# From the third batch on, two Fourier stages as 64x64 tiles of TensorE, eight groups a visit

## The chip, the cores and the metric

One core of one Trainium2 chip runs the whole program. The metric is the device time of one execution in microseconds. For the kernel before, three runs gave 746.88, 747.74 and 748.42 us, median 747.74. The profiled execution of the same kernel took 747.4 us; its span, from the first instruction to the last, is 745.2 us, so 2.2 us lie around it.

## The reference

Eight sequences of 3008 tokens with 256 features are filtered in the frequency domain, and the result goes through a two-layer network.

```
X = np.fft.rfft(x, axis=1)                  # x: (8, 3008, 256)
Y = X * (filt_r + 1j * filt_i)[None]        # filters: (1505, 256)
y = np.fft.irfft(Y, n=3008, axis=1)
h = y.reshape(24064, 256) @ w_in            # w_in: (256, 2048)
g = np.maximum(0.01 * h, h)
out = g @ w_out                             # w_out: (2048, 256)
```

## The kernel before

**The transform.** 3008 is 94 x 32, and each batch goes through four matmul stages in half precision:

- Stage 1 (`s1_group`, 16 groups, L259): a transform of length 94 over the rows, for two of the 32 values of n2 at a time. Its result is copied to half precision by ACT (L262) or DVE and stored in a DRAM scratch, `dz1` (L264).
- Stage 2 (`s2_group`, 12 groups): `t1_load` reads the scratch back, turned (L271), into `z1`, four slots of 128 partitions x 4 columns k1 x 256. Two matmuls of 128x128 weights by 256 columns (L308) fill one PSUM bank `pf`. DVE multiplies the bank by the two filter layouts, `fb_sb` (L317) and `fa_sb` (L320); the two 64-partition halves of the first product are exchanged by two transfers (L318, L319), and POOL adds the products into `y` (L323).
- Stage 3 (`sa_group`, 12 groups): one matmul of 128x128 weights by 512 columns on `y` (L330), copied by ACT (L332) and, after every second group, stored in the scratch `dz2` (L334).
- Stage 4 (`sb_group`, 16 groups): `t2_load` (L278) reads `dz2` back, four matmuls of 94 columns a group (L351), copied by ACT into `yt` (L341).

Batch 0 takes its own route, with DVE transposes in place of the scratch (`FIRST`), and a last part of it runs later (`late_sb`, L442). There, and in L401, weights of 128 rows by 64 columns are used in pairs that write the two halves of the PSUM partitions.

**The network.** The 24064 tokens are 47 chunks of 512. `moe1` multiplies by `w_in` (L514), 16 column tiles a chunk, two to a double bank `ph`; there are two of these, used in turn, and ACT applies the leaky relu and empties them (L519). The second product runs one chunk behind (L589; the first three chunks by L681), from the fourth chunk on by a Winograd-like scheme of seven products of 16 matmuls of 128 columns, with sums before (L555) and after them on DVE.

**The order.** It is written out by the program. Time is counted in units; a chunk is `SL = 8` units, a column tile of `moe1` falls every half unit, and 112 matmuls of the second product are spread evenly over the chunk. `at(time, f)` puts each piece of work into one list, which is emitted in order of time; each engine, and each queue of transfers, then runs in that order and waits only for what it needs. `PLANS` says when the groups of a batch begin and how far apart they are, 47 units a batch from the fourth on. A planner loop moves a group later until what it needs is there, at least `GAP = 0.6` units after the last; `load_time` places the reads back `LANDED = 2.43` units after the last store and `READ = 2.2` units ahead of their first use. The stage groups share two PSUM banks `pf`; the two `out_banks` and the two double banks `ph` belong to the network. SP issues nearly all transfers and runs through its list in order; POOL issues the loads of `x` and, at the start, of the weights and filters, which change from single to half precision on the way.

Units and microseconds: the first `moe1` matmul, at unit 0, starts at 34.27 us of the span; the first stage-4 group of batch 1, at unit 38.52, is at 109.24 us.

Of the kernel before, what the change touches and what calls it, by code (L numbers as in the profile page):

```python
# [11 lines left out]
P = 128  # L12
# [7 lines left out]
N1, N2 = 94, 32  # L20
NC = 24
Q = 32
R1 = 96
FP = 3


def _build_np_constants(N):
    n1, n2 = np.arange(N1), np.arange(N2)
    h = N2 // 2

    k2 = np.concatenate([np.arange(h), np.arange(N2 - 1, h - 1, -1)])

    sg = np.where(k2 < h, 1.0, -1.0)[None, :]
    th = 2 * np.pi * np.outer(n2, k2) / N2
    co, si = np.cos(th), np.sin(th)

    fwd1 = np.zeros((P, P))
    fwd2 = np.zeros((P, NC, P))
    inv1 = np.zeros((P, N2, N1))
    inv2 = np.zeros((P, P))  # L40

    for s, (qr, qi) in enumerate(((0, 2), (1, 3))):
        k1 = NC * s + np.arange(NC)

        cr, ci = (slice(64 * i + s, 64 * i + 64, 2) for i in range(2))
        r, i = (slice(Q * q, Q * q + Q) for q in (qr, qi))
        ang = 2 * np.pi * np.outer(n1, k1) / N1
        fwd1[:N1, qr * Q : qr * Q + NC] = np.cos(ang)
        fwd1[:N1, qi * Q : qi * Q + NC] = -np.sin(ang)
        for c in range(NC):  # L50
            t = th + 2 * np.pi * n2[:, None] * k1[c] / N
            fwd2[r, c, cr], fwd2[i, c, cr] = np.cos(t), np.sin(t)
            fwd2[r, c, ci], fwd2[i, c, ci] = -np.sin(t) * sg, np.cos(t) * sg

        w = np.where((k1 == 0) | (k1 == N1 // 2), 1.0, 2.0)[:, None] / N1
        for j in n2:
            t = ang.T + 2 * np.pi * j * k1[:, None] / N
            inv1[qr * Q : qr * Q + NC, j, :] = w * np.cos(t)
            inv1[qi * Q : qi * Q + NC, j, :] = -w * np.sin(t)
        inv2[cr, r], inv2[ci, r] = co.T, -(si * sg).T  # L60
        inv2[cr, i], inv2[ci, i] = si.T, (co * sg).T
    inv2 /= N2


    inv2r = np.concatenate([inv2[:64], -inv2[:64]], axis=0)
    inv2i = np.concatenate([inv2[64:], inv2[64:]], axis=0)
    small = np.stack([fwd1, inv2, inv2r, inv2i], axis=1)

    fwd2t = fwd2.reshape(4, Q, NC, P).transpose(1, 0, 2, 3).reshape(P, NC, P)
    inv1t = inv1.reshape(4, Q, N2, N1)[:, :NC].transpose(1, 0, 2, 3).reshape(4 * NC, N2, N1)  # L70
    fwd2 = fwd2.reshape(P, FP, NC // FP, P).transpose(1, 0, 2, 3)
    return tuple(np.ascontiguousarray(t).astype(np.float16) for t in (fwd2, inv1, small, fwd2t, inv1t))


@with_exitstack
def kernel(
# [28 lines left out]
    REST = (5.37, 14.61, 8.86, 10.48, 23.53, 20.72)  # L105
    DUE = (3.52, 0.66)
    TWICE = (2.2, 2.35)
    F2T = 3.24
    LEAD = (3.85, 7.37)
    AFTER = (0.53, 0.8, 1.33, 3.17, 0.39, 0.52)  # L110
# [2 lines left out]
    PLANS = (  # L113
        (0.68, 0.31, 12.95, 0.9, 4.35, 38.33, 2.78, 7.78, 1.61),
        (12.19, 1.53, 42.87, 2.62, 7.4, 85.59, 2.85, 16.13, 2.12),
        (40.7, 1.73, 77.28, 3.57, 5.62, 130.03, 2.65, -0.23, 2.52),
        (63.95, 2.85, 119.86, 3.87, 7.04, 177.42, 2.92, 12.93, 2.24),
    )

    f2_np, i1_np, small_np, f2t_np, i1t_np = _build_np_constants(N)  # L120
    f2_d = nc.inline_tensor(f2_np, name="fwd2_const")
    i1_d = nc.inline_tensor(i1_np, name="inv1_const")
    small_d = nc.inline_tensor(small_np, name="small_const")
    f2t_d = nc.inline_tensor(f2t_np, name="fwd2t_const")
    i1t_d = nc.inline_tensor(i1t_np, name="inv1t_const")

    cpool = ctx.enter_context(tc.tile_pool(name="const", bufs=1))
    f2_sb = cpool.tile([P, NC, P], FP16, name="f2_sb")
# [3 lines left out]
    fb_sb = cpool.tile([P, NC, D], FP16, name="fb_sb")  # L132
    w_in_sb = cpool.tile([P, NDT, DFF], FP16, name="w_in_sb")
    w_out_sb = cpool.tile([P, NCT, D], FP16, name="w_out_sb")
    wt_sb = cpool.tile([P, 4, NCH, P], FP16, name="wt_sb")
    x_sb = cpool.tile([P, N2, D], FP16, name="x_sb")
    big = [cpool.tile([P, Q * D], FP16, name=f"big{i}") for i in range(3)]
# [31 lines left out]
    def at(time, f):  # L169
        clock["n"] += 1  # L170
        heapq.heappush(work, (time, clock["n"], f))
# [69 lines left out]
    def turned(t, n, c):  # L241

        base = t[:]
        return bass.AP(tensor=base.tensor, offset=base.offset + 4 * c * D,
                       ap=[[P * D, n], [Q * D, 4], [1, 4 * D]])
# [22 lines left out]
    def t1_load(b, c):  # L268
        def go():
            need(*[("st1", b, h) for h in range(8)], *[("s2", b, 2 * c - 7)] * (c > 3))  # L270
            nc.sync.dma_start(z1[c % 4], turned(dz1[b % 2], N2, c))  # L271
            issued.add(("z1", b, c))
        return go

# [51 lines left out]
    def sa_group(b, g):  # L326
        def go():
            ps = bank("pf", 2, D)
            need(("y", b, g), *[("st2", b, g // 2 - 4)] * (g > 7))
            nc.tensor.matmul(ps, inv2, ys.pop((b, g))[:], start=True, stop=True)  # L330
            h = g // 2
            nc.scalar.copy(st2[h % 4][:, ds(2 * (g % 2), 2), :], ps)  # L332
            if g % 2:
                soon(AFTER[4], lambda: noted(("st2", b, h), lambda: nc.sync.dma_start(  # L334
                    dz2[b % 2][ds(4 * h, 4)].rearrange("k p d -> p k d"), st2[h % 4])))
        return go

    def quad_copy(h, dt, ps, copy):

# [354 lines left out]
    def plan(b, s1, s1_step, s2, s2_step, lag, sb, sb_step, xl, x_step):  # L694
        for g in range(16):
            groups.append((s1 + s1_step * g, 1, b, g, s1_group(b, g, dve if b == 1 and g % 4 < 3 else act)))
            if g % 2 and b + 1 < B:
                at(s1 + xl + x_step * g, lambda g=g: (need(("s1", b, g)), noted(
                    ("x", b + 1, g // 2), lambda: x_load(b + 1, 2 * g - 2, 4))))
        for g in range(12):  # L700
            groups.append((s2 + s2_step * g, 2, b, g, s2_group(b, g)))
            groups.append((s2 + lag + s2_step * g, 3, b, g, sa_group(b, g)))
        first_use[1, b], first_use[3, b] = s2, sb
        for g in range(16):
            due = SL * (QT * (8 * b + g // 2) // CH)
            groups.append((min(sb + sb_step * g, due - DUE[0] + DUE[1] * (g % 2)), 4, b, g, sb_group(b, g, act)))
# [21 lines left out]
    def load_time(stage, b, c):  # L728
# [7 lines left out]
            at(t, (t1_load if stage == 1 else t2_load)(b, c))  # L736
        return loads[stage, b, c]

    queue = [(time, n, *v) for n, (time, *v) in enumerate(groups)]
    heapq.heapify(queue)  # L740
    while queue:
        time, n, stage, b, g, f = heapq.heappop(queue)
        t = max(time, last + GAP)
        if stage == 3:
            behind = when[2, b, g] + y_delay(b, g) + 0.02 if (2, b, g) in when else None
        else:
            behind = load_time(stage - 1, b, g // 2) if stage != 1 else 0
            if stage != 1 and behind is not None:
                behind += READ
# [6 lines left out]
            place[stage - 1, g // 2 % 4] = t + 0.1  # L756
        assert stage < 4 or t < SL * (QT * (8 * b + g // 2) // CH), (b, g, t)

    for ci in range(NCHUNK + 1):
        if ci < NCHUNK:  # L760
            for ct in range(NCT):
                at(SL * ci + 0.5 * ct, lambda ci=ci, ct=ct: moe1(ci, ct))
        if ci == 0:
            continue
        wino = W0 <= ci - 1
# [39 lines left out]
```

## Time and profile before

| what | value | where from |
|---|---|---|
| median of three runs | 747.74 us | the runs |
| profiled execution, its span | 747.4 us, 745.2 us | the profiled run |
| PE busy | 738.0 us, 99% | part 1 of the page |
| DVE, ACT, POOL busy | 504.6, 559.1, 166.2 us | part 1 |
| granted TensorE clock | 0.999 | the spans of the cores |
| leaky relu, L519, 128x1024 | 376 x 1025 ns | groups by form |
| copies of stage 3, L332, 128x512 | 84 x 584 ns | groups by form |
| filter products, L317 and L320, 128x512 | 78 x 688 and 84 x 681 ns | groups by form |
| add of the products on POOL, L323 | 84 x 1388 ns | part 5 |
| load of x, landing after issue | 4.4 us for 192 KB | part 6 |

Busy times of PE are those of the records, whose modelled ends lie after the start of the next matmul; what one matmul costs in a stream is read from start to start. DMA issues on SP and POOL aren't counted as busy.

### The profile page before, as it was taken

Reading aid. Unit: us, or ns where it says so; the run is one execution under the profiler, and the core shown is the slowest. Engines: PE = TensorE matmul, PEld = TensorE weight load, DVE = VectorE, ACT = ScalarE, POOL = GpSimd, SP = SyncE. Lnnn points to the kernel's source line nnn. Section 1 sums busy time; section 2 is a strip of 40 time slices with the busy share of each in tenths; the row PEclk is TensorE's granted clock in tenths of the full one; section 3 lists DMA queues with packets and bytes.
Section 4 is the critical chain, followed back from the end, with each engine's and each line's share of the span. In section 5 each row is a group of like instructions: output and inputs, shape, how many; then the busy total and the mean of one; then the engine's idle time right before and its main releaser. Section 6 shows DMA issues by size and latency. Waiting matters only on the chain.

```text
span 745.2 us, 19416 instructions
## 1 busy us (share of the span) xinstructions
PE 738.0 (99%) x8017; PEld 528.9 (71%) x8017; DVE 504.6 (68%) x686; ACT 559.1 (75%) x755; POOL 166.2 (22%) x171
## 2 busy tenths in 40 slices
PE   9999999999999999999999999999999999999997
PEld 3556667677687777877778777777777777777776
DVE  5987637766776766766777667766677676465566
ACT  4776787888878787877777787787777777777762
POOL 6503412332232212121232222121212210000000
PEclk9999999999999999999999999999999999999999
DMA  9997797888876666655675656543554333111012
GB/s 207 229 224 197 191 224 216 209 195 208 216 181 147 159 186 176 169 138 163 193 178 150 159 155 175 156 139 109 144 160 119 106 103 103 60 55 55 29 46 70
DMA packets 119848, 113.64 MB, mean 152 GB/s; under 512 B 16384, under 2 KB 93056, under 8 KB 119568
## 3 DMA queue, kind: packets, MB, share of 16 engines
q1 hardware_dynamic: 104425, 94.73, 42.9%
q0 software_dynamic: 15056, 17.49, 15.8%
q8 instruction: 62, 1.02, 0.6%
q14 instruction: 26, 0.21, 0.1%
q10 hardware_dynamic: 279, 0.19, 0.1%
HBM read 57.51 MB, written 50.33 MB: 145 GB/s over the span
## 4 chain that ended last, share of the span: by engine, by line
PE 96%; DMA 1%; DVE 1%; ACT 1%; issue 0%; ACTq 0%; DVEq 0%
PE ph L514 43%; PE pf L589 18%; PE po_ps L589 18%; PE pf L259 3%; PE pf L351 3%; PE pf L308 2%; PE pf L330 2%; PE po_ps L373 1%; PE pf L681 1%; PE po_ps L681 1%; DMA dz<-big 1%; DMA big<-dz 0%; ACT yt L341 0%; PE pf L442 0%; PE ph L401 0%
## 5 line engine op out<-in xcount | busy, mean ns | idle before, releaser
L519 ACT ACTIVATE gt_c<-ph 128x1024 f16<-128x1024 f32 x376 | 385.3, 1025 | 133.5 <-PE ph L514 122.8
L514 PE MATMUL ph<-yt,w_in_sb 128*128 128x512 f16 (+7 forms) x1728 | 447.3, 351 | 0.2 <-ACT yt L341 0.2
L589 PEld LDWEIGHTS <-gt_c 128*128 128x128 f16 x2800 | 202.2, 98 | 91.1
L323 POOL TENSOR_TENSOR y_b_g<-p_b_g,p_b_g 128x512 f16<-128x512 f32 x84 | 116.4, 1388 | 414.9 <-DMA p_b_g<-p_b_g 249.9
L589 PEld LDWEIGHTS <-big 128*128 128x128 f16 x2128 | 151.2, 98 | 61.4
L514 PEld LDWEIGHTS <-w_in_sb 128*128 128x128 f16 x1728 | 137.5, 98 | 19.7 <-DVE yt L341 0.4
L317 DVE TENSOR_TENSOR p_b_g<-pf,fb_sb 128x512 f32<-128x512 f32 x78 | 53.7, 688 | 31.0 <-PE pf L308 13.8
L589 PE MATMUL po_ps<-wt_sb,gt_c 128*128 128x128 f16 x704 | 70.0, 219 | 0.0
L589 PE MATMUL pf<-wt_sb,gt_c 128*128 128x128 f16 x688 | 68.4, 219 | 0.0
L589 PE MATMUL pf<-w_out_sb,gt_c 128*128 128x128 f16 x720 | 67.9, 219 | 0.0
L589 PE MATMUL pf<-wt_sb,big 128*128 128x128 f16 x704 | 67.2, 219 | 0.0
L262 ACT CAST big<-pf 128x512 f16<-128x512 f32 x98 | 57.1, 588 | 11.9 <-PE pf L259 10.5
L589 PE MATMUL po_ps<-w_out_sb,gt_c 128*128 128x128 f16 x688 | 66.0, 219 | 0.0
L589 PE MATMUL po_ps<-wt_sb,big 128*128 128x128 f16 x688 | 65.3, 219 | 0.0
L341 ACT CAST yt<-pf 128x376 f16<-128x376 f32 x120 | 56.4, 473 | 10.9 <-PE pf L351 8.0
L555 DVE TENSOR_TENSOR big<-gt_c 128x2048 f16<-128x2048 f16 (+1 forms) x46 | 58.7, 1276 | 0.1
L555 DVE TENSOR_TENSOR gt_c<-gt_c 128x2048 f16<-128x2048 f16 x43 | 57.4, 1335 | 1.0
L320 DVE TENSOR_TENSOR p_b_g<-pf,fa_sb 128x512 f32<-128x512 f32 x84 | 57.2, 681 | 0.2
L555 DVE TENSOR_TENSOR big<-gt_c,big 128x2048 f16<-128x2048 f16 (+1 forms) x45 | 55.3, 1230 | 0.0
L555 DVE TENSOR_TENSOR big<-big,gt_c 128x2048 f16<-128x2048 f16 (+1 forms) x45 | 55.2, 1227 | 0.1
L332 ACT CAST big<-pf 128x512 f16<-128x512 f32 x84 | 49.0, 584 | 4.9 <-PE pf L330 3.0
L259 PE MATMUL pf<-x_sb,small_sb 94*128 94x512 f16 x109 | 41.6, 381 | 0.0
(97 smaller groups left out, 625.9 us busy)
## 6 DMA issues: line engine op xcount, KB each, us to landing
dz<-big SPq DMA_DIRECT2D x98, 256.0 KB
p_b_g<-p_b_g SPq DMA_DIRECT2D x156, 128.0 KB
out_dram<-ost_c_h SPq DMA_DIRECT2D x118, 128.0 KB
big<-dz SPq DMA_DIRECT2D x42, 256.0 KB
big<-dz SPq DMA_DIRECT2D x56, 192.0 KB
x_sb<-in_x_dram POOLq DMA_DIRECT2D x40, 192.0 KB, 4.4
x_sb<-in_x_dram POOLq DMA_DIRECT2D x2, 768.0 KB, 9.1
w_in_sb<-in_moe_w_in_dram POOLq DMA_DIRECT2D x1, 1024.0 KB, 13.2
```

The costliest lines, as they stand in the source:

```text
L259: nc.tensor.matmul(ps, fwd1[:N1], x_sb[:N1, ds(2 * g, 2), :], start=True, stop=True)
L262: copy(st[:, ds(2 * (g % 2), 2), :], ps)
L317: nc.vector.tensor_tensor(p2[:], ps, fb, AL.mult)
L320: nc.vector.tensor_tensor(p1[:], ps, fa, AL.mult)
L323: ("y", b, g), lambda: nc.gpsimd.tensor_tensor(y1[:], p1[:], p3[:], AL.add)))
L332: nc.scalar.copy(st2[h % 4][:, ds(2 * (g % 2), 2), :], ps)
L341: copy(yv, ps.rearrange("p c a -> p a c"))
L351: nc.tensor.matmul(ps[:, j, :], z2[h % 4][:K4, j, ts(dt, P)], i1_sb[:K4, 4 * h + j, :], start=True, stop=True)
L514: nc.tensor.matmul(ph[:, j, ds(t - ci * CH, e - t)], w_in_sb[:, dt, ts(ct, P)], yt[:, dt, ds(t % N, e - t)], start=(dt == 0), stop=(dt == ...
L519: nc.scalar.activation(gts[ci][:, ds(2 * g, 2), :], ph, AF.Lrelu)
L555: nc.vector.tensor_tensor(*(v[:, ds(c0, n)] for v in (o, i0, i1)), op)
L589: nc.tensor.matmul(of[t], a()[:, c, ts(t, P)], w[:, c, :], start=(c == 0), stop=(c == NCH - 1))
```

## The change

Batches 0 and 1 stay as they were. From batch 2 on (`QUARTERS = 2`) stages 2 and 3 are no longer placed as groups. The six `visit`s of a batch each do stage 2 for four columns k1 of each half of the spectrum (eight columns of 64 rows, where a group had two of 128) and, right behind it on PE, stage 3 of the visit before. In all there are 37 visits: the first has stage 2 alone and the last stage 3 alone.

- `forward`: eight matmuls with 64x64 weights by 256 columns; `s` picks the half of the contraction rows and the bank, `par` the half of the output partitions. It takes both `pf` banks.
- `filtered`: per half, two DVE products, two transfers that now exchange neighbouring partitions, one add on POOL: the same numbers as for two groups before. The second half is `SECOND = 1.05` units later.
- `backward`: four matmuls with 64x64 weights by 512 columns into a `ph` bank, one ACT copy of 128x1024, one store.
- `t1_load` makes two transfers of 64 partitions in place of one of 128.
- The rows of stage 1's result are reordered (real and imaginary part of a half next to each other), with the constants to match; the new weights `f2q` (384 KB) lie over the first half of `f2_sb`.
- The filters are loaded again in the new layout, in thirds (12, 6 and 6 of the 24 columns): per third eight loads by POOL, two copies from partition to partition by SP, and one product with a sign on DVE.
- The planner keeps other groups away from a visit (`AROUND`), and `moe1`'s tiles behind a visit are 0.35, 0.1 and 0.1 units later (`PAIRS`). Stage 1 of batch 3 has a step of 1.93 in place of 1.73.

```diff
+    QUARTERS = 2
+    VISITS = (44.75, 49.75, 55.75, 60.75, 65.75, 71.75) + tuple(8 * c + 4.75 for c in range(9, 40))
+    AROUND = (0.8, 1.15, 2.1)
+    HOLDS = (1.0, 2.0)
+    PAIRS = (0.35, 0.1, 0.1)
+    SECOND = 1.05
+    ADDED = 1.4
+    STORED = 1.2
+    REFILLED = 1.7
+    LATE = 46.5
...
-            nc.sync.dma_start(z1[c % 4], turned(dz1[b % 2], N2, c))
+            for s in range(2 if b >= QUARTERS else 0):
+                src = turned(dz1[b % 2], N2, c)
+                nc.sync.dma_start(z1[c % 4][ts(s, H)], bass.AP(
+                    tensor=src.tensor, offset=src.offset + 2 * s * Q * D, ap=[[P * D, N2], [Q * D, 2], [1, 4 * D]]))
+            if b < QUARTERS:
+                nc.sync.dma_start(z1[c % 4], turned(dz1[b % 2], N2, c))
...
+    def halves(v):
+        return v.rearrange("(k e) j d -> e k j d", e=2)
+    def refill(dst, src, q, par, k, first, sgn):
+        lo = H * par + Q * k
+        nc.gpsimd.dma_start(
+            halves(dst[lo : lo + Q, q])[0],
+            bass.AP(tensor=src.tensor, offset=src.offset + (first + sgn * (par + 2 * q.start)) * D,
+                    ap=[[N1 * D, N2 // 2], [sgn * 2 * D, q.stop - q.start], [1, D]]))
+    def both(t, q):
+        v = halves(t[:, q])
+        nc.sync.dma_start(v[1], v[0])
+    def refills(q, t):
+        for n in range(8):
+            dst, src = ((fb_sb, filt_i), (fa_sb, filt_r))[n // 4]
+            at(t + 0.4 * n, lambda v=(dst, src, q, n // 2 % 2, n % 2, *((0, 1), (N1, -1))[n % 2]): refill(*v))
+        at(t + 4.2, lambda: both(fb_sb, q))
+        at(t + 5.6, lambda: both(fa_sb, q))
+        at(t + 7, lambda: signed(q))
...
+            at(t, lambda: noted(("f2q",), lambda: nc.sync.dma_start(f2q, f2q_d.ap())))
+    def forward(b, v):
+        need(("z1", b, v), ("f2q",))
...
+        ps = [bank("pf", 2, D, hold) for hold in HOLDS]
+        for j in range(2):
+            for s in range(2):
+                for par in range(2):
+                    c = 2 * j + par
+                    nc.tensor.matmul(ps[s][ts(par, H), j, :], f2q[ts(s, H), 4 * v + c, :],
+                                     z1[v % 4][ts(s, H), c, :], start=True, stop=True)
+        for s in range(2):
+            if s:
+                soon(SECOND, lambda: filtered(b, v, 1, ps[1]))
+            else:
+                filtered(b, v, 0, ps[0])
+    def filtered(b, v, s, ps):
...
+        nc.vector.tensor_tensor(p2[:], ps, fb2[:, s, ds(2 * v, 2), :], AL.mult)
+        a, o = halves(p2[:]), halves(p3[:])
+        for e in range(2):
+            soon(AFTER[1], lambda e=e: nc.sync.dma_start(o[1 - e], a[e]))
+        nc.vector.tensor_tensor(p1[:], ps, fa2[:, s, ds(2 * v, 2), :], AL.mult)
...
+        soon(ADDED, lambda: noted(("yq", b, v, s), lambda: nc.gpsimd.tensor_tensor(y[:], p1[:], p3[:], AL.add)))
+    def backward(b, v):
...
+        ps = bank("ph", 2, CH)
+        y = [ys.pop((b, v, s)) for s in range(2)]
+        for par in range(2):
+            for s in range(2):
+                nc.tensor.matmul(ps[ts(s, H), par, :], i2q_sb[ts(par, H), :],
+                                 y[s][ts(par, H)].rearrange("p j d -> p (j d)"), start=True, stop=True)
+        nc.scalar.copy(st2[v % 4].rearrange("p (j w) d -> p w j d", w=2), ps.rearrange("p w (j d) -> p w j d", j=2))
+        soon(STORED, lambda: noted(("st2", b, v), lambda: nc.sync.dma_start(
+            dz2[b % 2][ds(4 * v, 4)].rearrange("k p d -> p k d"), st2[v % 4])))
+    def visit(i):
+        b, v = QUARTERS + i // 6, i % 6
+        if b < B:
+            forward(b, v)
+        if i:
+            backward(b - (v == 0), (v - 1) % 6)
...
+        for v in visits:
+            if -AROUND[0] < t - v < AROUND[1] or AROUND[1] < t - v < AROUND[2] and last > v:
+                t = v + AROUND[1 if last < v else 2]
...
+    for lo, hi, t in ((0, 12, 0), (12, 18, 0), (18, 24, LATE)):
+        refills(slice(lo, hi), max(t, when[2, 1, hi // 2 - 1] + REFILLED))
...
+    for t in visits[1:]:
+        for n, v in enumerate(PAIRS):
+            later[2 * int(t) + 2 + n] = v
...
-                at(SL * ci + 0.5 * ct, lambda ci=ci, ct=ct: moe1(ci, ct))
+                at(SL * ci + 0.5 * ct + later.get(NCT * ci + ct, 0), lambda ci=ci, ct=ct: moe1(ci, ct))
```

## The prediction

> **What bounds the kernel now.** I read the page's busy times and slices first, then the groups by form, then PE's timeline, where starts tell what a matmul costs, and last the chain of waits and the DMA share where the change adds transfers.
>
> ```profile
> span 745.2 us, 19416 instructions
> ## 1 busy us (share of the span) xinstructions
> PE 738.0 (99%) x8017; PEld 528.9 (71%) x8017; DVE 504.6 (68%) x686; ACT 559.1 (75%) x755; POOL 166.2 (22%) x171
> ...
> DMA  9997797888876666655675656543554333111012
> ...
> q1 hardware_dynamic: 104425, 94.73, 42.9%
> q0 software_dynamic: 15056, 17.49, 15.8%
> ...
> PE 96%; DMA 1%; DVE 1%; ACT 1%; issue 0%; ACTq 0%; DVEq 0%
> ```
>
> PE is the bound: 99% busy and 96% of the chain. What leaves PE's stream shortens the kernel if nothing new stops PE; ACT and DVE have room. In slices of 18.6 us the DMA engines have little room before 112 us (the first six) and much later.
>
> PE's timeline, around 310 us and where batch 0 uses weights of 64 columns:
>
> ```profile
> 309.82 0.38 PE L330 MATMUL pf<-y_b_g,small_sb 128*128 128x512 f16 x1
> 310.03 0.22 PE L589 MATMUL po_ps<-wt_sb,big 128*128 128x128 f16 x1
> ...
> 310.92 0.38 PE L308 MATMUL pf<-big,f_sb 128*128 128x256 f16 x2
> 311.14 0.60 PE L514 MATMUL ph<-yt,w_in_sb 128*128 128x320 f16 x4
> ```
>
> ```profile
> 16.79 0.39 PE L397 MATMUL ph<-big,f_sb 128*128 128x128 f16 x4 [0.50 <-issue]
> 17.11 0.42 PE L401 MATMUL pf<-big,f_sb 128*64 128x128 f16 x8
> 17.46 0.39 PE L373 MATMUL po_ps<-idle 128*128 128x512 f16 x1
> ```
>
> From start to start a group's L330 costs 0.216 us and its two L308 0.218 us. In the second fence L397 is four full matmuls of 128 columns, 0.056 each, so the next should start at 17.02; L401 starts at 17.11. Its eight matmuls of half the weight columns are four pairs; four pairs at 0.056 would end at 17.335, and the next full matmul starts at 17.46. So pairs do overlap (eight in the time of four), and going into this shape and out again costs 17.46 - 17.02 - 0.224 = 0.22 us. The mid-stream case at 58.74 us (L442, eight of 94 columns) agrees: 0.47 us from 58.65 to 59.12, of which four pairs are 0.25 at their distance of 0.063.
>
> **The change, part by part.**
>
> *PE per visit.* Removed: two groups of stage 2 and two of stage 3, 2 x 0.218 + 2 x 0.216 = 0.868 us. Added: eight 64x64 matmuls by 256 columns, four at a time in the four quarters of the array, so two rounds of 0.109; four by 512 columns, one round of 0.216; one way in and out for both, since `backward` follows `forward` directly: 0.22. Sum 0.654. Saved: 0.214 a visit. 35 visits have both parts: 7.5 us. The first (0.218 + 0.22 against 0.436) and the last (0.216 + 0.22 against 0.432) save nothing.
>
> That the two row halves overlap as the column halves do is shown by no row; the pairs of L401 even read the same moving data. Bounds: if only pairs overlap, a visit is 0.436 + 0.432 + 0.22 = 1.09, a loss of 7.8 us in 36; if the switch were free, 0.434, a gain of 15.2 in 35. I take the value with four at a time and the full switch, since row and column halves write separate banks and partitions here.
>
> The Trainium skill speaks against the change (TensorEngine Tiling (Array Packing), Key Properties): changing the tiling mode drains TensorE. The trace agrees, with 0.09 us in front of L401 and the rest of 0.22 behind. The skill (TensorE: Matmul & The Clock Gate, Measured speedup vs the span model) also has four row tiles only 3.07 times as fast, not four. By that figure, an estimate, a visit is 2 x 0.868 / 3.07 + 0.22 = 0.785, and the saving is 2.9 us; the pairs of L401 come to 2 x 0.056 / 0.058 = 1.9 of 2.
>
> *ACT.* Two L332 of 584 ns become one copy of 128x1024, like an L519: 1025 ns. 5 us less, hidden, as PE is the bound. What matters is the `ph` bank it takes. The next `moe1` pair needs the other bank, whose relu was just asked for: a relu starts 0.42 us after the start of its pair's last matmul (58.32 to 58.74), takes 1.025, and PE goes on 0.05 after a release (64.92 to 64.97 us, ACT to L308): 1.50 us. Meanwhile PE has that matmul 0.216, twelve product matmuls between units 4.5 and 5.35 at 0.056, and the visit 0.654: 1.54. It just fits, by 0.04 us, thanks to the 0.35 of `PAIRS`. I take 0 for it; without that cover each 0.1 us is 3.5 us in all.
>
> *DVE, POOL, `pf`.* The same four products and two adds a visit. The first `pf` bank is free after about 0.5 + 0.69 + 0.68 = 1.9 us; the next group is 1.15 units, some 2.2 us, behind. In 33 visits, at unit 4.75 of the chunk, DVE's sums (L555, 1.23 to 1.34 us) begin at 4 and are done. Four of batch 2 fall at 1.75 or 7.75, where a sum or a product's add is in front: up to 0.3 us late each, at most 1.2. I take 0.5 for them. The y of a visit is read by the next one, at least 5 units (10 us) later; an exchange issued at 306.94 us before was added from 311.09 on, so I take 0.
>
> *SP.* 36 more issues of about 0.5 us; `z1` is asked for 4.85 units before use at the earliest: 0. The steady DMA share falls from 0.69 (300 to 316 us) to 0.30: nothing is late there.
>
> *The filters and `f2q`.* Before the first visit (unit 44.75, about 121 us) two thirds of the filters are reloaded. In PE's times the loads are from about 74 to 91 us, the copies at 83, 86, 93 and 96, `f2q` at 93, and there the profile has its only near-edge chain after the start:
>
> ```profile
> 100.17 0.50 ACT big L332
> 100.67 0.02 issue
> 100.69 5.51 DMA dz<-big
> 106.20 0.02 issue
> 106.21 2.98 DMA big<-dz
> 109.20 0.05 issue
> 109.24 0.35 PE pf L351 x4
> ```
>
> ```profile
> core 0: us, PE busy (x) PEld busy (x) DVE busy (x) ACT busy (x) POOL busy (x), PEclk, DMA share, GB/s
> ...
> 75.00:93.00 18.00, 18.00 (x129) 11.80 (x127) 11.28 (x20) 13.70 (x18) 8.92 (x9) 1.00 0.78 195
> 93.00:110.00 17.00, 16.84 (x151) 10.86 (x150) 6.96 (x10) 15.60 (x25) 3.28 (x6) 1.00 0.92 216
> ```
>
> The last store of stage 3 of batch 1, the read back and the first stage-4 matmul follow each other without slack (0.2 us of PE idle); a transfer that is late here stops PE. Added bytes: eight loads of 16 x 12 x 512 B and eight of half that, 1.18 MB, at q0's price (15.8% of 745.2 us for 17.49 MB) 7.9 us of all engines; copies 1.18 MB and `f2q` 0.39 MB at q1's price (42.9% for 94.73 MB) 5.3 us. Sum 13.2. Free: 0.22 x 18 + 0.08 x 17 = 5.3. So up to 7.9 us could fall on the chain. The lower end is 0: most added transfers are issued 5 to 25 us ahead of the store, and what is delayed may have slack. I take 2.0, nearer the lower end, since only the tail of the backlog meets the store. POOL issues 16 loads of about 0.55 us (as L196) in gaps of 3.3 to 4.7 us between batch 1's adds; the y's they delay by 1 to 2 us are used 3 us later. The last third comes at unit 46.5, DMA share 0.81, needed at 60.75: 0.
>
> **Sum:** 747.4 (profiled execution) - 7.5 + 0.5 + 2.0 = 742.4 us. The profiled execution is 0.34 below the median of the runs, 747.74.
>
> **The rivals.**
>
> *The copies block SP's queue (slower).* `both` waits in SP's list for the loads; the stores and reads of the chain above are behind it. Loads of filters and x between 74 and 100 us are 1.18 + 0.79 = 1.97 MB on q0. At the rate at which 1 MB of `w_in` landed (13.2 us) they end at 99 us, before the store; at that of a load of x (192 KB in 4.4 us) at 119. From a rate of 60 GB/s on (107 us) the store is over 7 us late and the gain is gone; at 55, some 10 us late, 750. For: queue and chain have no slack. Against: q0's loads overlap, so 4.4 us each is too much.
>
> *Only pairs overlap.* 747.4 + 7.8 + 0.5 + 2.0 = 757.7. For: no row shows row halves. Against: weights, banks and partitions are separate.
>
> *Part of the overlap or of the cover fails.* 0.15 us more a visit, by weights loaded one behind the other (L442's distance of 0.063 us where 94 columns need 0.039) or by the margin of 0.04 us at `ph`: 35 x 0.15 = 5.3, so 747.7: no change. For: the margin. Against: L401's 0.058. The skill's 3.07 belongs here: by its saving of 2.9 us the time would be 747.0.
>
> **Chances.** Forecast 0.68, blocked queue 0.13, pairs only 0.06, part 0.13. What this measurement can tell from no change is 0.2%, 1.5 us. The part case splits 0.05 faster, 0.06 same, 0.02 slower. Faster 0.73, same 0.06, slower 0.21. Forecast's own range 738.5 to 745: from no wait at all and a switch of 0.18 us (747.4 - 8.9) to 5 us at the hand-over. For 8 in 10 it reaches to the part case and the blocked queue: 738.5 to 750.
>
> **What would show it.** Right: PE at 99%, the eight and four 64x64 matmuls in three rounds, a visit of 0.65 us from the matmul before to the one behind; no PE idle at L514 behind a visit; at 100 to 110 us an idle of about 2 us before L351. Wrong: rounds that start 0.2 us or more apart where 0.109 is expected; ACT releasing L514 in each chunk; SP waiting long at the copies with PE idle near 109 us.

## The result, and the profile after

The changed kernel takes 756.01 us (median of 4 runs, 753.77 to 757.12), the kernel before 747.65 beside it (4 runs, 746.88 to 748.42). The ratio is 1.0108, with a 95% interval of 1.0083 to 1.0134: 8.4 us slower, where 742.4 was forecast. The profiled execution is the one of 757.12 us, the slowest of the four.

The head of its page (busy us and share of the span; then the slices of PE and of its granted clock, and the shares of the chain that ended last):

```profile
span 755.3 us, 19901 instructions
...
PE 736.3 (97%) x8233; PEld 519.6 (69%) x8233; DVE 527.1 (70%) x689; ACT 552.4 (73%) x719; POOL 180.8 (24%) x195
...
PE   8999988989999999999999999999999999999997
...
PEclk9999999989999999999999999999999999999999
...
PE 91%; DMA 5%; DVE 1%; ACT 1%; issue 0%; POOL 0%; SPq 0%; POOLq 0%; DVEq 0%; ACTq 0%
```

PE is 1.7 us less busy than before (736.3 to 738.0), and the span is 10.1 us longer: PE has less to do and waits more. Its slices, of 18.9 us each, show where: the 8s in slices 6, 7 and 9 (94 to 132 us and 151 to 170 us), with the clock's only 8 in slice 9. The chain has 5% of DMA in place of 1%.

The same visit that was costed, in PE's timeline of the changed kernel (start, us, instructions):

```profile
408.37 0.33 PE L699 MATMUL po_ps<-wt_sb,big 128*128 128x128 f16 x3
408.63 0.41 PE L411 MATMUL pf<-big,f_sb 64*64 64x256 f16 x8
408.87 0.39 PE L435 MATMUL ph<-y_b_v,i2q_sb 64*64 64x512 f16 x4
409.19 0.62 PE L699 MATMUL po_ps<-wt_sb,big 128*128 128x128 f16 x8
```

Three matmuls at 0.056 from 408.37 leave the next due at 408.54. `forward` starts at 408.63, `backward` 0.24 us behind it, and the next full matmul at 409.19: 409.19 - 408.54 = 0.65 us for the visit, as forecast (0.654). (A visit stands for two groups of stage 2 and two of stage 3; the eight of the title are its columns k1.) By the starts in the trace, 33 of the 35 visits with both parts cost 0.654 us; of the others, the one at 151.40 us waits for its y, and the one at 199.13 costs 1.23, with its tiles coming apart by 0.38 and 0.28 us.

The stretches in which the forecast looked for trouble (length; busy us of PE, PEld, DVE, ACT, POOL; granted clock; DMA share; GB/s):

```profile
core 0: us, PE busy (x) PEld busy (x) DVE busy (x) ACT busy (x) POOL busy (x), PEclk, DMA share, GB/s
75.00:93.00 18.00, 17.94 (x128) 11.78 (x126) 12.32 (x20) 13.43 (x18) 11.50 (x16) 1.00 1.05 222
93.00:110.00 17.00, 13.98 (x112) 8.62 (x111) 6.60 (x9) 13.19 (x21) 7.29 (x10) 1.00 1.10 265
110.00:130.00 20.00, 17.64 (x201) 12.70 (x199) 8.98 (x13) 12.06 (x16) 1.00 (x2) 0.91 0.79 208
130.00:160.00 30.00, 25.24 (x266) 17.16 (x265) 19.51 (x27) 18.74 (x25) 11.64 (x17) 0.90 0.84 200
```

Against the lines shown of before, the DMA share rises from 0.78 to 1.05 and from 0.92 to 1.10, PE loses 3 us from 93 to 110 and more after that, and behind 110 us the clock is 0.91 and 0.90.

Who waited for whom from 74 to 160 us (us in total, times, longest):

```profile
DVE fb_sb L386 <- DMA fb_sb<-fb_sb: 8.7, 2, 5.4
...
PE ph L435 <- POOL y_b_v L427: 3.1, 1, 3.1
...
PE pf L461 <- DMA big<-dz: 2.4, 1, 2.4
...
PE po_ps L699 <- DVE gt_c L665: 1.9, 1, 1.9
...
PE pf L699 <- DVE big L752: 1.6, 1, 1.6
...
PE pf L359 <- POOL y_b_g L352: 1.1, 2, 0.6
```

PE's own waits are the five lower lines: 10.1 us, of which before had 0.2. The top line stands behind two of them. DVE's timeline (in square brackets the idle time before, and what ended it):

```profile
105.08 0.62 DVE L386 TENSOR_SCALAR fb_sb<-fb_sb,sign_sb 128x1536 f16<-128x1536 f16 x1 [5.41 <-DMA fb_sb<-fb_sb]
105.62 1.22 DVE L665 TENSOR_TENSOR gt_c<-gt_c 128x2048 f16<-128x2048 f16 x1
...
148.09 0.97 DVE L386 TENSOR_SCALAR fb_sb<-fb_sb,sign_sb 128x1536 f16<-128x1536 f16 x1 [3.29 <-DMA fb_sb<-fb_sb]
```

The product with the sign is the next instruction in DVE's list, its copy has not landed, and DVE stands. Behind it wait the sums L665, for which PE waits until 106.89 us, and the second time L752, for which PE waits until 149.72. The chain also goes through that copy, but not through DVE (start, us, engine, what, line):

```profile
98.60 5.85 DMA fb_sb<-fb_sb
...
105.49 6.74 DMA dz<-big
...
112.31 3.21 DMA big<-dz
...
115.57 0.35 PE pf L461 x4
```

These lines answer to the chain at 100.17 to 109.24 us of before: the hand-over from stage 3 to stage 4. The store takes 6.74 us in place of 5.51, the read back 3.21 in place of 2.98, and the first stage-4 matmul starts at 115.57: 6.3 us late, of which 4.8 are the issue of the store (105.49 for 100.69). What it stores was ready 1.6 us late, at 102.28, and then stood 3.2 us in SP's list. The copies stand ahead of it there, and at them SP had waited for their loads (us in total, times, longest, from 74 to 160 us; the 3.1 of the first line come later, at the last third):

```profile
SPq L382 <- DMA fb_sb<-in_filt_i_dram: 3.6, 2, 3.1
SPq L382 <- DMA fa_sb<-in_filt_r_dram: 3.1, 2, 2.1
```

Later, in batch 2, the chain goes through the exchanges:

```profile
140.44 6.78 DMA p_b_v<-p_b_v
...
148.95 4.73 DMA p_b_v<-p_b_v
153.85 1.27 POOL y_b_v L427
...
155.16 0.64 PE ph L435 x3
```

An exchange takes 6.78 and 4.73 us to land, and `backward` waits 3.1 us for the y of the visit before it. This, too, is SP's list. The second half's product starts on DVE at 141.73 and takes 0.68 us. Its exchange is issued 6 us later, from 148.37 on, behind a copy of the last third, at which SP waits 3.1 us for the loads, and four stores:

```profile
139.81 1.73 SPq L424 DMA_DIRECT2D p_b_v<-p_b_v  x2
144.75 0.47 SPq L382 DMA_DIRECT2D fb_sb<-fb_sb  x1
...
148.37 1.17 SPq L424 DMA_DIRECT2D p_b_v<-p_b_v  x2
```

The granted clock around the two longest of PE's waits, 2.36 us until 115.57 and 3.14 us until 155.16:

```profile
116.00:118.00 2.00, 2.00 (x19) 1.50 (x17) 0.42 (x1) 0.90 (x2) 0.00 (x0) 0.62 1.02 302
118.00:120.00 2.00, 2.00 (x14) 1.27 (x13) 0.56 (x1) 1.02 (x1) 0.00 (x0) 0.52 0.39 104
...
156.00:158.00 2.00, 2.00 (x15) 1.43 (x13) 1.74 (x2) 0.87 (x1) 0.09 (x1) 0.50 0.89 124
158.00:160.00 2.00, 2.00 (x15) 1.35 (x13) 2.00 (x4) 1.02 (x2) 0.00 (x0) 0.50 0.85 214
160.00:162.00 2.00, 2.00 (x16) 1.19 (x15) 0.42 (x1) 1.00 (x4) 0.01 (x1) 0.78 0.69 218
```

PE runs on at half speed for some 3.4 and 5.7 us. Lost are 2 x (0.38 + 0.48) = 1.7 us and 2 x (0.50 + 0.50 + 0.22) = 2.4 us, and 0.4 us between 155.16 and 156, where the clock was 0.51: 4.5 us in all.

Last, how late PE stands, by the same `moe1` matmul in two traces. Each column is the matmul that starts at that time in the profiled execution of before, each number how much later (us) it starts in the other kernel's profiled execution:

```
at (us), before     90    112    141    170    182    250    400    550    700
after             +0.4   +8.0   +9.2  +15.1  +15.1  +14.6  +11.9  +10.3   +9.9
no_reload         -0.3   -0.2   +1.1   +3.2   +3.2   +2.7   +0.1   -1.6   -2.0
no_copies         -0.4   +0.3   +2.9   +5.0   +5.0   +4.5   +1.9   +0.2   -0.2
no_late           -0.1   +7.2   +8.4  +10.5  +10.5  +10.1   +7.4   +5.8   +5.4
copies_later      +0.2   +4.7   +6.0   +7.4   +7.4   +7.0   +4.3   +2.6   +2.2
from_fourth       +0.3   +4.2   +4.1   +4.1   +4.1  +14.9  +12.3  +10.6  +10.2
from_fifth        +1.3   +4.8   +4.8   +4.8   +4.8   +5.9   +3.8   +2.1   +1.7
```

The profiled executions took 757.1, 745.1, 746.9, 752.7, 749.4, 757.4 and 749.0 us, in the order of these rows, which isn't always near the median of the runs. The whole loss of the changed kernel lies between 90 and 170 us. From 182 to 700 us it gains 15.1 - 9.9 = 5.2 us in the 30 visits that have both parts, from batch 3's first on: 0.17 each. The visit at 199.13 us is one of the 30; without its 0.58 us it would be 0.19.

### The profile page after: what moved, and what is told of

Read it like the earlier page. It is cut to its first block, busy times and chain, and to the rows that moved or that the text cites. A ratio compares the mean times of both kernels' runs of the same rounds, so it can differ in the third digit from the quotient of the medians.

```text
span 755.3 us, 19901 instructions
## 1 busy us (share of the span) xinstructions
PE 736.3 (97%) x8233; PEld 519.6 (69%) x8233; DVE 527.1 (70%) x689; ACT 552.4 (73%) x719; POOL 180.8 (24%) x195
## 3 DMA queue, kind: packets, MB, share of 16 engines
q8 instruction: 64, 1.05, 0.6%
## 4 chain that ended last, share of the span: by engine, by line
PE 91%; DMA 5%; DVE 1%; ACT 1%; issue 0%; POOL 0%; SPq 0%; POOLq 0%; DVEq 0%; ACTq 0%
PE ph L624 42%; PE pf L699 18%; PE po_ps L699 18%; PE pf L283 3%; PE pf L461 3%; PE pf L411 2%; DMA p_b_v<-p_b_v 2%; PE pf L791 1%; PE po_ps L791 1%; PE ph L435 1%; DMA dz<-big 1%; DMA big<-dz 1%; DMA fb_sb<-fb_sb 1%; DMA big<-in_x_dram 1%; PE po_ps L483 1%
## 5 line engine op out<-in xcount | busy, mean ns | idle before, releaser
L624 PE MATMUL ph<-yt,w_in_sb 128*128 128x512 f16 (+7 forms) x1728 | 449.5, 353 | 0.2 <-ACT yt L451 0.2
L699 PEld LDWEIGHTS <-gt_c 128*128 128x128 f16 x2800 | 199.1, 98 | 94.3 <-DVE gt_c L665 2.1
L699 PEld LDWEIGHTS <-big 128*128 128x128 f16 x2128 | 146.5, 98 | 70.5 <-issue 14.1
L427 POOL TENSOR_TENSOR y_b_v<-p_b_v,p_b_v 128x512 f16<-128x512 f32 x72 | 103.0, 1431 | 380.8 <-DMA p_b_v<-p_b_v 209.5
L624 PEld LDWEIGHTS <-w_in_sb 128*128 128x128 f16 x1728 | 136.8, 98 | 17.0 <-issue 1.3
L665 DVE TENSOR_TENSOR gt_c<-gt_c 128x2048 f16<-128x2048 f16 x43 | 67.3, 1565 | 1.4
L699 PE MATMUL pf<-wt_sb,gt_c 128*128 128x128 f16 x688 | 66.0, 219 | 0.0
L665 DVE TENSOR_TENSOR big<-gt_c 128x2048 f16<-128x2048 f16 (+1 forms) x46 | 64.5, 1402 | 0.3
L286 ACT CAST big<-pf 128x512 f16<-128x512 f32 x98 | 57.0, 583 | 8.7 <-PE pf L283 7.6
L665 DVE TENSOR_TENSOR big<-big,gt_c 128x2048 f16<-128x2048 f16 (+1 forms) x45 | 56.2, 1249 | 0.1
L421 DVE TENSOR_TENSOR p_b_v<-pf,fb_sb 128x512 f32<-128x512 f32 x72 | 49.3, 685 | 7.7 <-PE pf L411 4.2
L665 DVE TENSOR_TENSOR big<-gt_c,big 128x2048 f16<-128x2048 f16 (+1 forms) x45 | 54.0, 1201 | 0.0
L425 DVE TENSOR_TENSOR p_b_v<-pf,fa_sb 128x512 f32<-128x512 f32 x72 | 48.9, 680 | 0.0
L461 PE MATMUL pf<-i_sb,big 96*128 96x94 f16 x448 | 38.4, 207 | 2.4 <-DMA big<-dz 2.4
```

Source lines behind the costliest of these rows:

```text
L286: copy(st[:, ds(2 * (g % 2), 2), :], ps)
L421: nc.vector.tensor_tensor(p2[:], ps, fb2[:, s, ds(2 * v, 2), :], AL.mult)
L425: nc.vector.tensor_tensor(p1[:], ps, fa2[:, s, ds(2 * v, 2), :], AL.mult)
L427: soon(ADDED, lambda: noted(("yq", b, v, s), lambda: nc.gpsimd.tensor_tensor(y[:], p1[:], p3[:], AL.add)))
L461: nc.tensor.matmul(ps[:, j, :], z2[h % 4][:K4, j, ts(dt, P)], i1_sb[:K4, 4 * h + j, :], start=True, stop=True)
L624: nc.tensor.matmul(ph[:, j, ds(t - ci * CH, e - t)], w_in_sb[:, dt, ts(ct, P)], yt[:, dt, ds(t % N, e - t)], start=(dt == 0), stop=(dt == ...
```

## The experiments

The runs of one group shared a chip, and each ratio is to the kernel before on that chip, whose medians lie from 747.69 to 747.99.

**What the reload costs.** Four runs: the changed kernel without the whole reload, without its copies and sign products, without its last third, and with all of it in place but the copies at other units.

`no_reload`:

```diff
-        for n in range(8):
-            dst, src = ((fb_sb, filt_i), (fa_sb, filt_r))[n // 4]
-            at(t + 0.4 * n, lambda v=(dst, src, q, n // 2 % 2, n % 2, *((0, 1), (N1, -1))[n % 2]): refill(*v))
-        at(t + 4.2, lambda: both(fb_sb, q))
-        at(t + 5.6, lambda: both(fa_sb, q))
-        at(t + 7, lambda: signed(q))
```

> Leaves out the whole reload of the filters: the 24 loads, the 6 copies and the 3 sign products (f2q and the other new weights still come), so the products from batch 2 on use filters in the old layout. Theory (the reload costs the early stalls, the visits themselves gain): the changed kernel's stalls between 92 and 156 us, some 15 us, go; 740 to 742.5 us, and the gaps before the products and stage 3 near 107 and 155 us are gone. Rival (something else in the visits or in the moved tiles stops PE early, and the reload only stands beside it): 750 or more.

Measured: 744.77 us (743.56 to 745.07, 4 runs), ratio 0.9947 (0.993 to 0.9964). Faster than before by 2.9 us, and 11.2 below the changed kernel: the reload costs more than the whole loss. What is left is 2 us short of what the theory expected at the worst. Three waits for y in batch 2 hold it back, 3.2 us in all:

```profile
PE ph L429 <- POOL y_b_v L421: 3.2, 3, 1.5
```

They stand without any reload, and so belong to the visits of batch 2, which are 5 and 6 units apart (`from_fourth` below, whose visits are 8 units apart, has no wait for a y of a visit). SP's issues around the first of them, and then its first product, its adds on POOL and the `backward` behind them:

```profile
113.81 5.07 SPq L297 DMA_DIRECT2D big<-dz  x8
118.99 4.45 SPq L679 DMA_DIRECT2D out_dram<-ost_c_h  x5
...
125.52 2.45 SPq L418 DMA_DIRECT2D p_b_v<-p_b_v  x4
```

```profile
120.76 0.69 DVE L415 TENSOR_TENSOR p_b_v<-pf,fb_sb 128x512 f32<-128x512 f32 x1
...
128.40 3.49 POOL L421 TENSOR_TENSOR y_b_v<-p_b_v,p_b_v 128x512 f16<-128x512 f32 x2 [10.38 <-DMA p_b_v<-p_b_v]
...
131.94 0.41 PE L429 MATMUL ph<-y_b_v,i2q_sb 64*64 64x512 f16 x3 [1.52 <-POOL y_b_v L421]
```

The first product is done at 121.45, and its exchange is issued 4 us later, from 125.52 on. SP was still at the five stores of results, late behind the eight half reads of `z1`, and then had one more store and two more half reads ahead of it. The adds start at 128.40 and end at 131.89: `backward` was due 1.5 us before.

`no_copies`:

```diff
-        at(t + 4.2, lambda: both(fb_sb, q))
-        at(t + 5.6, lambda: both(fa_sb, q))
-        at(t + 7, lambda: signed(q))
```

> Keeps the 24 loads, leaves out the 6 partition copies on SP and the 3 sign products on DVE, so half of the filter rows stay in the old layout. Theory (queues: SP's list stands at the copies, DVE's at the sign products, and PE behind DVE): 741 to 744 us. Rival (traffic: the loads' bytes slow the transfers of batch 1 to 2, the waits of the queues are their effect): 749 to 755 us, with stage 4's first read back near 112 us as late as in the changed kernel.

Measured: 746.66 us (745.76 to 747.97, 10 runs), ratio 0.998 (0.997 to 0.9991). Between the two expectations; stage 4's first read back is waited for 0.9 us, until 109.54, and not until 115.57. The loads alone cost 746.66 - 744.77 = 1.9 us; the copies and the sign products, on top of them, 756.01 - 746.66 = 9.3.

`no_late`:

```diff
     def refills(q, t):
+        if q.stop == NC:
+            return
```

> Leaves out the reload of the last third alone (8 loads, 2 copies, 1 sign product at units 46.5 to 53.5); those filters stay in the old layout. By the trace of the changed kernel the chunks from 142 to 174 us lose 7 to 8 us more against before. Theory (the third is to blame for its own place): 747 to 749.5 us. Rival (these stalls are an after-effect of the first two thirds, PE and the queues being late): 753 us or more.

Measured: 750.64 us (748.24 to 752.68, 10 runs), ratio 1.0037 (1.0022 to 1.0051). That is 1.1 us above the theory's range and below the rival's. The last third, which the forecast had at nothing, costs 5.4 us. The table above shows where: this run follows the changed kernel to 141 us (+8.4 beside +9.2) and is 4.6 us ahead at 170. It also shows which part weighs more in the first two thirds: PE is 7.2 us late at 112, and of its waits until then 1.3 us stand behind a sign product, but 3.6 are for the read back.

`copies_later`:

```diff
-        at(t + 4.2, lambda: both(fb_sb, q))
-        at(t + 5.6, lambda: both(fa_sb, q))
-        at(t + 7, lambda: signed(q))
+        c = 37 if t < 40 else 54
+        at(c, lambda: both(fb_sb, q))
+        at(c + 1, lambda: both(fa_sb, q))
+        at(c + 4.2, lambda: signed(q))
```

> All the work of the change, but copies and sign products stand later: for the first two thirds the copies at units 37 and 38 and the sign product at 41.2, behind the read back of stage 3; for the last third at 54, 55 and 58.2. Theory (queues): as without the copies, 741 to 745 us, faster than the kernel before. Rival (traffic): 749 to 755 us.

Measured: 749.42 us (747.58 to 751.96, 10 runs), ratio 1.0019 (1.0004 to 1.0034). By its time this is the rival's range: it stays slower than before. Still, the same bytes and the same instructions cost 6.6 us less than in the changed kernel, so most of what copies and sign products cost is not how many bytes they move, but when and where they stand. That the lists are a part of it shows in the last store of stage 3 of batch 1. SP issues it at 105.49 us in the changed kernel and at 105.73 in `no_late`, where the copies stand ahead of it, and at 100.40, 100.30 and 100.89 in `no_reload`, `no_copies` and here (100.69 before). Full DMA engines alone did not delay it: from 75 to 93 us their share is 1.09 in `no_copies` and 1.08 here, 1.05 in the changed kernel. Whether the rest of the 6.6 us is the lists or the traffic at that time isn't separated. These waits of PE are left from 74 to 160 us:

```profile
PE ph L436 <- POOL y_b_v L428: 2.6, 3, 1.6
PE pf L462 <- DMA big<-dz: 2.2, 1, 2.2
```

The first line is the wait for y of `no_reload`. The second is the hand-over to stage 4, and not the copies' doing: the store takes 8.36 us to land, the read back is issued at 109.27, and the first copy only at 111.67. Up to there SP issues the same as in `no_copies`, where that wait is 0.9 us.

**Why y is late in batch 2.** A theory of SP's issue time against one of full DMA engines. `halves_by_pool` is `copies_later` with half of the row-half reads of the first four columns of batch 2 issued by POOL:

```diff
-                nc.sync.dma_start(z1[c % 4][ts(s, H)], bass.AP(
+                (nc.gpsimd if s and b == QUARTERS and c < 4 else nc.sync).dma_start(z1[c % 4][ts(s, H)], bass.AP(
```

> As copies_later, but the second halves of the first four z1 reads of batch 2 are issued by POOL in place of SP; nothing else changes. In copies_later SP issues eight of these half reads one behind the other at some 0.6 us each, and the exchanges of the first visit stand behind them; its y is read 1.6 us too late by the second visit (at 137 us). Theory (SP's issue time makes the first y late): that wait falls from 1.6 to under 0.5 us, 747.5 to 748.5 us in all. Rival (the exchange itself lands late, since the DMA engines are full): the wait stays over 1.2 us, 749 to 750 us.

Measured: 749.18 us (747.26 to 751.96, 10 runs), ratio 1.0013 (0.9999 to 1.0028), no different from `copies_later`. The stretch from 120 to 130 us, first here, then in `copies_later`:

```profile
120.00:130.00 10.00, 10.00 (x130) 7.28 (x128) 7.43 (x12) 7.15 (x11) 1.63 (x4) 1.00 1.01 262
```

```profile
120.00:130.00 10.00, 10.00 (x137) 7.53 (x136) 7.99 (x12) 7.09 (x10) 1.00 (x2) 1.00 0.81 208
```

The DMA share (the last but one number) rises from 0.81 to 1.01: the reads come sooner and fill the engines. SP issued the exchanges from 127.19 on, 3 us sooner than in `copies_later` (130.21), but the first add starts 4.55 us behind that and not 3.03. PE waits 0.8 us until 133.22 and 1.9 until 135.51 for the two y of this visit, where `copies_later` waits 1.6 us until 136.86. The theory that SP's issue time alone makes y late isn't borne out; full DMA engines fit, but no run took bytes alone away here.

**The visits from a later batch on.** `from_fourth` leaves batch 2 as it was before (31 visits), with the reload behind batch 2's stage 2:

```diff
-    QUARTERS = 2
-    VISITS = (44.75, 49.75, 55.75, 60.75, 65.75, 71.75) + tuple(8 * c + 4.75 for c in range(9, 40))
+    QUARTERS = 3
+    VISITS = tuple(8 * c + 4.75 for c in range(9, 40))
...
-    LATE = 46.5
+    LATE = 82
...
+        at(t + 5.5, lambda: both(fb_sb, q))
+        at(t + 7, lambda: both(fa_sb, q))
+        at(t + 9.5, lambda: signed(q))
...
+            t = when[2, 2, 11] + REFILLED
...
```

> The same visits from the fourth batch on alone (QUARTERS = 3, 31 visits): batch 2 keeps its groups, the filters are reloaded behind its stage 2 (units 57 to 90), stage 1 of batch 3 has its step of 1.73 again, the copies stand 5.5 and 7 and the sign product 9.5 units behind the start of a third. All the change's kinds of work are there. Theory (the early stalls come from where the reload and the dense visits of batch 2 fall, the visits gain 0.15 us each as in the steady part of the trace): 31 x 0.15 = 4.7 us less than before, at most 1.5 of it lost; 742.5 to 744.5 us. Rival (any reload next to running stages costs its 5 to 10 us): 748 us or more.

Measured: 755.85 us (754.45 to 757.72, 5 runs), ratio 1.0106 (1.0087 to 1.0124). The theory's range is missed by 11 us. One wait explains nearly all of it, the weights `f2q` at the first visit, which SP's queue reached too late (SP's issue first, then PE's wait):

```profile
194.91 0.45 SPq L400 DMA_DIRECT2D f_sb<-fwd2q_const  x1
```

```profile
PE pf L411 <- DMA f_sb<-fwd2q_const: 10.2, 1, 10.2
```

The table shows the step, from +4.1 at 182 us to +14.9 at 250. So `from_fourth_early` asks for `f2q` some 14 units sooner:

```diff
-        at(t + 9.5, lambda: signed(q))
+        at(76.2 if q.start == 12 else t + 9.5, lambda: signed(q))
...
-            t = when[2, 2, 11] + REFILLED
+            t = when[2, 2, 5] + REFILLED + 2
```

> As from_fourth, whose first visit stood 10.2 us for the new weights f2q, issued by SP at 194.9 us behind everything else; here f2q and the small weights stand some 14 units earlier (behind group 5 of batch 2, whose half of the old weights they overwrite), and the sign product of the second third at unit 76.2. Theory (the visits gain 0.15 us each, the losses are the queue's): the wait goes, 743 to 746 us. Rival (SP's backlog stops PE at the first visits in another way, by the reads of z1 or the exchanges): 748 us or more.

Measured: 750.61 us (747.37 to 756.28, 12 runs), ratio 1.0039 (1.0018 to 1.0059): by its time the rival. The wait for `f2q` is gone. In its place, in a profiled execution of 755.36 us, PE waits 5.0 us at 212 us for the read back of batch 2's stage 4, where the last third's copies now stand, and 4.5 us in four smaller waits from 111 to 192 us. `from_fourth_thin` loads in quarters, two of them behind that read back, and asks for `f2q` at unit 60:

```diff
-    for lo, hi, t in ((0, 12, 0), (12, 18, 0), (18, 24, LATE)):
+    for lo, hi, *times in ((0, 6, 56, 61.5, 66), (12, 18, 66.7, 70.9, 75.2), (6, 12, 87.2, 93.2, 97), (18, 24, 91, 96, 99.5)):
```

(the three numbers behind a quarter's columns are the units of its loads, its copies and its sign product)

> As from_fourth_early, which lost 5.0 us at a read back of stage 4 (212 us, with the copies of the last third issued there) and some 3 more before and at the first visits; here the reload is in quarters, the two that only visits 3 to 5 need stand behind that read back (units 87 to 97), and the copies have more time. Theory (places, not the amount): 743.5 to 746 us. Rival (the bytes): 748 us or more.

Measured: 750.37 us (748.2 to 753.95, 12 runs), ratio 1.0038 (1.0025 to 1.0052). The theory fell. The profiled execution took 753.95 us. PE's longest waits in it from 100 to 260 us are two, at 112 and at 212:

```profile
PE pf L460 <- DMA big<-dz: 5.3, 2, 3.3
```

The second only fell from 5.0 to 3.3 us; a y of stage 3 is waited for another 1.6 us until 197.27. What still makes that read back late wasn't settled.

`from_fifth` has visits from batch 4 on alone (25), and half as long again for the reload (units 97 to 146, where it was 20 to 53), in quarters:

```diff
+    QUARTERS = 4
+    VISITS = tuple(8 * c + 4.75 for c in range(15, 40))
...
+            t = 99
...
+    for lo, hi, *times in ((0, 6, 97, 103, 107), (12, 18, 108, 113.5, 117.5), (6, 12, 132, 138, 142), (18, 24, 137, 143, 146.5)):
```

> The visits from the fifth batch on alone (QUARTERS = 4, 25 visits). The filters are reloaded in quarters, two of them (columns 0 to 5 and 12 to 17) before the first visit and two 25 to 40 units later, each with 5.5 to 6 units from the first load to the copies and 4 more to the sign product; f2q 25 units ahead of its use. Theory (the visits gain 0.15 us each; the reload costs only where its copies and sign products wait in SP's and DVE's queues, or its traffic meets a read back that PE waits for): 25 x 0.15 = 3.8 us less than before, at most 1.5 of it lost, 744 to 745.5 us. Rival (a reload beside running stages always stops PE for some 5 us): 748 us or more.

Measured: 745.67 us (743.91 to 749.0, 6 runs), ratio 0.9964 (0.9952 to 0.9976): 0.2 us above the theory's range, and faster than the kernel before by 2.1 us and than the changed kernel by 10.3. The profiled execution took 749.0 us, and even in that PE waits only twice for more than 0.3 us from 100 to 260 us, here and 0.9 us for a y at 243:

```profile
PE pf L460 <- DMA big<-dz: 2.1, 1, 2.1
```

This is the hand-over at 112 us, a hundred us before the first load of the change.

**The hand-over in the unchanged kernel.** That first wait had been 0.2 us in the profile of before. Two runs asked whether the profile or the program differs: the kernel before once more, and the kernel before with the two small tiles that the change adds, unused:

```diff
+    i2q_sb = cpool.tile([P, 64], FP16, name="i2q_sb")
+    sign_sb = cpool.tile([P, 1], FP32, name="sign_sb")
```

> The kernel before, profiled once more. The profile that the prediction was made from has 0.2 us of PE idle where stage 4 of batch 1 waits for its first read back (109 us); from_fourth, which is the same program up to there, had 2.4 us. Theory (this wait differs from execution to execution, whatever the change): another 0.3 to 3 us here, with a span to match. Rival (it does not differ, and something in the changed programs' start makes it): 0.2 us again.

> The kernel before with two small tiles more in SBUF in front of the large ones, as the change has them (132 bytes a partition), set to zero once and used nowhere. from_fourth and from_fourth_early, the same program up to unit 57, waited 2.4 and 1.7 us at 111 us for stage 4's first read back; the kernel before did not in two profiles. Theory (where the tiles lie makes the transfers there later): 1.5 us or more of PE idle near 110 us, 749 us. Rival (it is not the place of the tiles): under 0.5 us, 747 to 748.5 us.

Measured: 747.66 us (746.52 to 748.47, 8 runs), ratio 0.9997, and 747.87 (746.92 to 749.75, 8 runs), ratio 1.0003 (0.9992 to 1.0013). The place of the tiles costs nothing in the median. The wait itself was 0 in one profile and 1.24 us at 110.26 in the other (between the two expectations), beside 0.2 in the first: it differs from execution to execution. That it was 1.7 to 2.4 in the profiles of the three `from_fourth` runs and of `from_fifth` may be more than that; their instructions are those of before up to this point, and its cause stays open, as it does for the 2.2 of `copies_later`.

## Why the prediction was wrong

By the runs the 8.4 us are put together like this:

| term | forecast | measured | from |
|---|---|---|---|
| 35 visits on PE | -7.5 | -6.0 | 0.17 each (the table of starts) |
| waits for y in batch 2 | 0 (+0.5 for late banks) | +3.2 | `no_reload`'s waits |
| loads of the reload | in the 2.0 | +1.9 | `no_copies` less `no_reload` |
| copies and sign products | in the 2.0; 0 for the last third | +9.3 | the changed kernel less `no_copies` |
| sum | -5.0 | +8.4 | |

The first two lines give -2.8 where `no_reload` has 744.77 - 747.69 = -2.9 in its medians (-1.9 in the spans of the profiled executions). The lines for the reload are differences of runs in this one order; in another order the shares could come out otherwise.

*PE per visit: right.* Four tiles of 64x64 do run side by side, a visit is 0.65 us, and the rival in which only pairs overlap is refuted. Over many visits the gain is 0.17 each and not 0.214, although the matmuls of 29 of these 30 visits cost the 0.654 of the forecast; half of the difference is the one visit at 199.13 us, and where the other 0.02 of a visit goes is not known. That the measured 756.0 lies nearest to the 757.7 of the pairs-only rival is chance. The Trainium skill's 3.07 for four row tiles (TensorE: Matmul & The Clock Gate, Measured speedup vs the span model), which would have made a visit 0.785, isn't what these 64x64 tiles do.

*ACT and the `ph` bank: right.* The margin of 0.04 us held: over the whole run PE waits 0.2 us at L624, once, as it did before.

*"The y of a visit is read by the next one, at least 5 units (10 us) later ... so I take 0": failed.* The zero rested on one exchange from a quiet stretch, 4.2 us. In batch 2, products, SP's queue, exchanges and two adds took 131.94 - 120.76 = 11.2 us, 1.5 more than there were (`no_reload`). This cost 3.2 us. SP's list (4 us from product to exchange) and the two adds (3.5 us) had no term.

*"I take 2.0, nearer the lower end, since only the tail of the backlog meets the store": the main failure.* The place was right, and so was an idle time of about 2 us in front of stage 4 (2.36). But PE was 8.0 us late at 112 us, 7.6 of it since 90. That this is near the upper end of 7.9 us is chance: the term was sized by bytes against free DMA time, and the loads, nearly half of the added bytes, cost 1.9 us over the whole kernel. What the runs show in its place are two lists that run in order. The copies wait in SP's list for the loads, and the store of stage 3 behind them is issued 4.8 us late, and 5.0 in `no_late`; in the three runs without copies there it is on time. The sign product waits in DVE's list for the copies and held DVE for 5.4 and 3.3 us, of which PE waited 1.9 and 1.6. With the same bytes in other places, `copies_later` is 6.6 us faster. So the rival of the copies that block SP's queue named the larger part of the mechanism, and its sign, SP waiting long at the copies, is there. Its 750 us had no sign product and no last third; without the last third the kernel takes 750.6.

*"The last third comes at unit 46.5, DMA share 0.81, needed at 60.75: 0": failed.* It was asked when the filters are needed, not what is queued behind their copies and their sign product. It costs 5.4 us (`no_late`): PE waits 1.6 us until 149.72 behind DVE's 3.3, and 3.1 until 155.16 for an exchange that SP issued 6 us behind its product, with half the clock after it.

*A term that was missing: the clock.* The forecast let a wait cost its own length. The waits of 2.4 and 3.1 us had some 3.4 and 5.7 us at half clock behind them, 4.5 us lost in all. PE's waits (10.1) and the half clock (4.5) make 14.6 of the 14.7 us that the changed kernel lost from 90 to 182 us; since the five visits with both parts there gained about 1, some 1 us more lies in idle times too short to be listed.

What stays open: the wait of 3.3 us at batch 2's read back in `from_fourth_thin`, and why the hand-over waited 1.7 to 2.4 us in versions that had changed nothing up to there.

## What to carry to other kernels

Cost a one-time rearrangement by what is queued behind each of its instructions on its in-order engine, not by its bytes: a copy that waits in SP's list for a load, or a short DVE product that waits for the copy, costs all that stands behind it, and is put far enough behind that it never waits. On an engine that is 99% busy, a wait can cost more than its length by the clock: 1.7 and 2.9 us more behind waits of 2.4 and 3.1. And a gain per visit is worth taking only in the stretches that have room for it: with the rearrangement two batches later and spread out, 25 visits gained 2.1 us where 37 with it in the way lost 8.4.

## What the runs showed of the hardware

- Four 64x64 tiles on the two row and the two column halves start within 10 ns of each other (in 33 of the 35 visits with both parts), in rounds 0.11 to 0.13 us apart for 256 columns. Row halves with different moving data overlap as column halves do.
- SP needs no less time to issue a transfer of half the partitions. The read of a column before, and two row halves of it after:

```profile
113.40 1.76 SPq L271 DMA_DIRECT2D big<-dz  x4
```

```profile
118.64 5.09 SPq L297 DMA_DIRECT2D big<-dz  x8
```

1.76 / 4 = 0.44 us for 128 partitions, 5.09 / 8 = 0.64 us for 64: a column costs SP 1.27 us in place of 0.44.

- The clock fell to half behind idle times of 2.36 and 3.14 us, and not behind the one of 1.95 us that ended at 106.89. The Trainium skill (TensorE: Matmul & The Clock Gate, What's actually happening) has it fall after one idle window of about 3.4 us whose place is not tied to the kernel; here less idle time than a whole window was enough. The length alone didn't decide: a wait of 1.96 us until 112.10 in `from_fourth_thin` had the half clock behind it (0.61 and 0.54 in the next 4 us), one of 2.25 us until 111.31 in `halves_by_pool` had not (1.00).
- The kernel before shows waits of 0, 0.2 and (with two unused tiles) 1.24 us at the same place in three profiled executions, while its medians agree within 0.03%. A wait of one profile is a sample.
